# Four weight loads on one queue: moving a tap load and the projection load of a gated convolution to ScalarE's DMA queue

## The chip, the cores and the metric

The kernel runs on one core of a Trainium2 chip. A core has five engines with instruction streams of their own: TensorE (PE: matrix products into PSUM; its weight loads are shown apart, as PEld), VectorE (DVE), ScalarE (ACT), GpSimd (POOL) and SyncE (SP), which here only starts transfers. Transfers between HBM and the core's SBUF are done by 16 DMA engines. SyncE and ScalarE both start transfers in this kernel, each with an instruction in its own stream; the profile lists SyncE's transfers under the DMA queue q1 and ScalarE's under q10. The metric is the device time of one execution in microseconds (us), as the median of several runs.

## The reference

The inputs are `x` (2 x 16000 x 256, bf16), three taps `w` (3 x 256 x 512) and a projection `w_o` (256 x 256). It is a causal convolution over time with dilation 2, a gate and a projection:

```
h[t] = x[t] @ w[0] + x[t-2] @ w[1] + x[t-4] @ w[2]     (x before time 0 is zero)
f, g = the first and the last 256 columns of h
out  = (tanh(f) * sigmoid(g)) @ w_o
```

## The kernel before, in words

**Tiling.** Time is read in rows of four steps, t = 4r + j with j from 0 to 3, so that `x` of a batch has 4000 rows. A group is up to 256 such rows; there are 34 groups, and the first has 128 rows. Each group is made in four blocks of 128 output columns (two of f, two of g), 136 blocks in all. In SBUF `x` lies transposed (`xt`: input channels on the partitions, rows along the free dimension), because the products contract over channels. The steps j = 0, 1 of all rows of a block go to one PSUM bank (`a`), the steps j = 2, 3 to another (`b`).

**Two ways to a block.** The first group (blocks 0 to 3) is made directly: each bank adds the products of all three taps, tap 2 first, then tap 0, then tap 1 (`TAPS = (2, 0, 1)`, function `direct`, line 216). All later blocks use fewer products (function `products`, line 197): VectorE forms a difference `mm` (line 155) and a sum `pp` (line 161) of shifted rows, VectorE or GpSimd differences `dd` (line 172), and TensorE multiplies them by combined weights: `wm_sb` = w[0] + w[2] - w[1], `wp_sb` = w[0] + w[2] + w[1], and `wd0_sb`, `wd2_sb` = twice w[0] and w[2]. VectorE puts the results together (lines 234 and 235) after ScalarE has copied one bank (line 227). ScalarE applies tanh and sigmoid (line 248), VectorE multiplies them (line 266), TensorE projects with `wo_sb` (line 287), ScalarE evicts (line 306), and SyncE stores (line 308).

**How the combined weights come about.** ScalarE makes `wd0_sb` (line 363, needs w[0]) and `wd2_sb` (line 364, needs w[2]). VectorE makes `wt_sb` = w[0] + w[2] (line 365, needs those two), then `wm_sb` (line 366) and `wp_sb` (line 367), which need w[1] as well. Behind these three, in VectorE's stream, stand `mm` and `pp` of group 1 (lines 155, 161), which need the first transposed chunk.

**Loading.** `x` is loaded in chunks. The rows of chunk 0 (the first group) come as a plain copy (`xn`, line 117) and are transposed by TensorE with an identity (line 141); ScalarE and VectorE copy the result to `xt` (line 143, j even and j odd). All other chunks are loaded by a transposing DMA that SyncE starts (line 105). Chunk 1 has 256 rows and 16 rows of history (0.56 MB), chunk 2 and most others 512 and 16 (1.08 MB). Chunks 1 and 2 are started at once, since three buffers of `xt` are there; later ones wait for a buffer to come free. Each tap is 256 KB and `w_o` 128 KB, plain copies.

**The order at the start.** The kernel is in manual order: each engine runs its instructions as the text has them. At the start TensorE runs 28 small products on a zeroed tile (`warm_up`, line 92), then the transposes, one more small product, and the first group's products: 12 with tap 2, 12 with tap 0, 12 with tap 1 for blocks 0 to 2, then block 3's taps 2 and 0, the `wm` and `wp` products of block 4, and block 3's tap 1. ScalarE starts two tap loads (line 119), loads its activation table (line 120), and comes to its copies of line 143. SyncE starts `xn` (line 117), tap 0 (line 121) and then the transposing loads. The load of `w_o` is in ScalarE's stream behind its first activations of block 0 (line 375).

Of the kernel before, what the change touches and what calls it, by code (L numbers as in the profile page):

```python
# [13 lines left out]
def kernel(  # L14
# [19 lines left out]
    nc = tc.nc  # L34
# [4 lines left out]
    P = 128  # L39
# [7 lines left out]
    TAPS = (2, 0, 1)  # L47
# [41 lines left out]
    def warm_up(n):  # L89
        wps = ps_a.tile([P, 2 * RG], f32, name="a")  # L90
        for _ in range(n):
            nc.tensor.matmul(wps[:, :P], lhsT=warm[:], rhs=warm[:], start=True, stop=True)  # L92
# [20 lines left out]
    w_taps = [consts.tile([P, CT, D2], bf16, name=f"w{k}_sb") for k in range(K)]  # L113
    wo_sb = consts.tile([P, NT, D], bf16)
    xn = consts.tile([P, 4, D], bf16, name="xn")
    w_in = [w[k].rearrange("(ct c) d -> c ct d", c=P) for k in range(K)]
    nc.sync.dma_start(out=xn[:], in_=x[0, 0:4 * P, :].rearrange("(r j) c -> r j c", j=4))
    for k in (TAPS[0], TAPS[2]):
        nc.scalar.dma_start(out=w_taps[k][:], in_=w_in[k])
    nc.scalar.preload_act_table(ACT.Sigmoid)  # L120
    nc.sync.dma_start(out=w_taps[TAPS[1]][:], in_=w_in[TAPS[1]])
    warm_up(N_WARM[0])
    ident = consts.tile([P, P], bf16)
    make_identity(nc, ident[:])
# [56 lines left out]
    def products(k, which):  # L181
        g, oi = divmod(k, 4)
        G = groups[g]
        o = O_ORDER[oi]
        osl = slice(o * P, (o + 1) * P)
        R = G["R"]
        N = 2 * R
        if which in (1, 2):
            G["ab"[which - 1], oi] = (ps_a, ps_b)[which - 1].tile([P, 2 * RG], f32, name="ab"[which - 1])
        wmat, mv, bank, first = {  # L190
            2: (wm_sb, lambda ct: G["m"][:, :, ct, :R], "b", True),
            1: (wp_sb, lambda ct: G["p"][:, :, ct, :R], "a", True),
            3: (wd0_sb, lambda ct: G["d"][:, 2:4, ct, :R], "b", False),
            0: (wd2_sb, lambda ct: G["d"][:, 0:2, ct, :R], "a", False),
        }[which]
        for ct in range(CT):
            nc.tensor.matmul(  # L197
                G[bank, oi][:, :N], lhsT=wmat[:, ct, osl], rhs=mv(ct),
                start=first and ct == 0, stop=ct == CT - 1, skip_group_check=True,
            )  # L200
# [21 lines left out]
    def copy_m2(k):  # L222
        g, oi = divmod(k, 4)
        G = groups[g]
        N = 2 * G["R"]
        G["ss", oi] = ss_pool.tile([P, 2 * RG], f32, name="ss")
        nc.scalar.copy(out=G["ss", oi][:, :N], in_=G["b", oi][:, :N])  # L227
# [9 lines left out]
    def activate(k):  # L237
        g, oi = divmod(k, 4)
        G = groups[g]
        R = G["R"]  # L240
        o = O_ORDER[oi]
        if oi == 0:
            G["th"] = act_pool.tile([P, NT, 4, RG], bf16, name="th")
            G["sg"] = act_pool.tile([P, NT, 4, RG], bf16, name="sg")
            G["z"] = z_pool.tile([P, NT, 4, RG], bf16, name="zz")
        dst = G["th"][:, o] if o < NT else G["sg"][:, o - NT]
        for h, bank in ((1, "b"), (0, "a")):
            nc.scalar.activation(  # L248
                out=dst[:, 2 * h:2 * h + 2, :R],
                in_=G[bank, oi][:, :2 * R].rearrange("p (q r) -> p q r", q=2),  # L250
                func=ACT.Tanh if o < NT else ACT.Sigmoid, scale=1.0 if g == 0 else 0.5,
            )
# [118 lines left out]
    direct(3, TAPS[:-1])  # L371
    products(N_DIRECT, 2)
    products(N_DIRECT, 1)
    activate(0)
    nc.scalar.dma_start(out=wo_sb[:], in_=w_o.rearrange("(ct c) d -> c ct d", c=P))
    activate(1)
    activate(2)
    copy_m2(N_DIRECT)
    for part in range(3):
        last = pre_d(1, part, nc.vector)  # L380
# [8 lines left out]
    k = N_DIRECT + 1  # L389
# [76 lines left out]
```

## Time and profile before

| what | value |
|---|---|
| median of 3 runs (all) | 284.21 us (284.19, 284.21, 284.81) |
| the profiled execution | 284.75 us; its span 283.0 us |
| TensorE busy | 278.2 us, 98% of the span |
| ScalarE, VectorE, GpSimd busy | 261.2, 243.2, 126.2 us |
| bytes on SyncE's queue q1 and ScalarE's q10 | 33.59 MB and 0.66 MB |
| plain loads, from issue to landing (median) | taps on ScalarE 4.3 us, tap on SyncE 4.5 us, `xn` 2.9 us, `w_o` 4.1 us |
| transposing loads, from issue to landing (median) | 6.8 us |

The span is the time from the first to the last instruction in the profile; the profiled execution's own time is 1.75 us longer, for what lies around it. In a line of the timeline the first number is the start in us from the span's start and the second is how long it took; ACTq and SPq are the instructions by which ScalarE and SyncE start a transfer, which end when the transfer is handed over and not when the data has landed. In a line of a DMA queue the three numbers are packets, MB, and the packets' time as a share of 16 engines' time in the stretch; the share goes over 100% where packets overlap. A transposing load moves packets of 256 bytes, a tap load packets of 1 KB, `xn` of 2 KB, `w_o` of 512 bytes, and at the end of each transfer 4-byte packets set its semaphore.

### The profile page before, as it was taken

The page shows a single profiled execution, that of the slowest core. Times are in us where ns is not written, and L with a number is a line of the kernel's source. Part 1 is how long each engine was busy: PE and PEld are TensorE (multiplying, and loading weights), DVE is VectorE, ACT ScalarE, POOL GpSimd, SP SyncE. Part 2 cuts the span into 40 slices and gives each one's busy share as a digit, 9 for nine tenths or more (in the row PEclk, how much of TensorE's full clock was granted, in tenths as well). Part 3 has the DMA queues.
Part 4 walks back from the last instruction along what each step waited for, and adds up shares of the span by engine and source line. Part 5 has one row for each costly group of instructions (what it writes and reads, how often), then busy time and mean ns, then how long its engine had stood idle before and what let it go on. Part 6 is the DMA issues. An engine that isn't in the chain of part 4 may idle for free.

```text
span 283.0 us, 4903 instructions
## 1 busy us (share of the span) xinstructions
PE 278.2 (98%) x1641; PEld 160.5 (57%) x1641; DVE 243.2 (86%) x417; ACT 261.2 (92%) x533; POOL 126.2 (45%) x136
## 2 busy tenths in 40 slices
PE   8999999999999999999999999999999999999994
PEld 7645555555555555556854555555555555555782
DVE  2999888888888888888999988888888888888884
ACT  4699999999999999999999999999999999999994
POOL 1145455445444544543465544454445445443430
PEclk9999999999999999999999999999999999999999
DMA  8877191632828252182793714709355152321223
GB/s 206 195 174 168 58 210 74 153 113 82 182 76 151 88 115 75 41 222 76 177 257 96 166 41 122 179 37 171 127 124 149 45 156 76 79 75 74 76 87 110
DMA packets 76440, 34.55 MB, mean 122 GB/s; under 512 B 66944, under 2 KB 68480, under 8 KB 76416
## 3 DMA queue, kind: packets, MB, share of 16 engines
q1 hardware_dynamic: 75600, 33.59, 47.5%
q10 hardware_dynamic: 816, 0.66, 0.7%
q8 instruction: 13, 0.21, 0.3%
q14 instruction: 11, 0.09, 0.1%
HBM read 1.18 MB, written 16.38 MB: 62 GB/s over the span
## 4 chain that ended last, share of the span: by engine, by line
PE 98%; DVE 0%; DVEq 0%; issue 0%
PE a L197 38%; PE b L197 38%; PE o_ps L287 19%; PE a L216 1%; PE a L92 1%; PE b L216 1%; PE tp L141 0%; PE a L332 0%; DVE osb_end L339 0%; PE b L332 0%; DVEq L461 0%; DVE warm L112 0%
## 5 line engine op out<-in xcount | busy, mean ns | idle before, releaser
L172 POOL TENSOR_TENSOR dd<-xt 128x512 bf16<-128x512 bf16 (+2 forms) x128 | 125.4, 980 | 146.7 <-DVE zz L266 65.4
L234 DVE TENSOR_TENSOR b<-a,ss 128x512 f32<-128x512 f32 (+2 forms) x132 | 87.4, 662 | 30.9 <-ACT ss L227 27.8
L235 DVE TENSOR_TENSOR a<-a,ss 128x512 f32<-128x512 f32 (+2 forms) x132 | 86.2, 653 | 0.0
L227 ACT COPY ss<-b 128x512 f32<-128x512 f32 (+2 forms) x132 | 73.8, 559 | 11.9 <-PE b L197 1.1
L197 PEld LDWEIGHTS <-wd_sb 128*128 128x128 bf16 x528 | 51.4, 98 | 55.1 <-issue 0.6
L197 PE MATMUL a<-dd,wd_sb 128*128 128x512 bf16 (+2 forms) x264 | 74.7, 364 | 0.0
L197 PE MATMUL b<-mm,wm_sb 128*128 128x512 bf16 (+2 forms) x264 | 74.7, 364 | 0.0
L197 PE MATMUL a<-pp,wp_sb 128*128 128x512 bf16 (+2 forms) x264 | 74.7, 364 | 0.0
L197 PE MATMUL b<-dd,wd_sb 128*128 128x512 bf16 (+2 forms) x264 | 74.7, 364 | 0.0
L287 PE MATMUL o_ps<-wo_sb,zz 128*128 128x256 bf16 x488 | 73.2, 273 | 0.0
L306 ACT CAST osb<-o_ps 128x512 bf16<-128x512 f32 x121 | 71.9, 594 | 0.0
L287 PEld LDWEIGHTS <-zz 128*128 128x128 bf16 x488 | 47.7, 98 | 28.2
L266 DVE TENSOR_TENSOR zz<-th,sg 128x1024 bf16<-128x1024 bf16 (+1 forms) x67 | 43.1, 644 | 0.0
L248 ACT ACTIVATE th<-b 128x512 bf16<-128x512 f32 (+2 forms) x68 | 39.7, 584 | 2.0 <-PE b L216 1.4
L197 PEld LDWEIGHTS <-wp_sb 128*128 128x128 bf16 x264 | 25.8, 98 | 27.3
L248 ACT ACTIVATE sg<-b 128x512 bf16<-128x512 f32 (+2 forms) x68 | 39.6, 582 | 0.6 <-PE b L197 0.3
L248 ACT ACTIVATE th<-a 128x512 bf16<-128x512 f32 (+2 forms) x68 | 39.7, 584 | 0.0
L248 ACT ACTIVATE sg<-a 128x512 bf16<-128x512 f32 (+2 forms) x68 | 39.7, 583 | 0.0
L197 PEld LDWEIGHTS <-wm_sb 128*128 128x128 bf16 x264 | 25.8, 98 | 4.5
L161 DVE TENSOR_TENSOR pp<-xt 128x1024 bf16<-128x1024 bf16 (+2 forms) x33 | 21.9, 662 | 0.0
L155 DVE TENSOR_TENSOR mm<-xt 128x1024 bf16<-128x1024 bf16 (+2 forms) x33 | 21.5, 650 | 0.0
L216 PEld LDWEIGHTS <-w_sb 128*128 128x128 bf16 x48 | 4.9, 105 | 1.4 <-issue 0.2
(35 smaller groups left out, 37.5 us busy)
## 6 DMA issues: line engine op xcount, KB each, us to landing
out_dram<-osb SPq DMA_DIRECT2D x61, 256.0 KB, 2.1
w_sb<-in_w_dram ACTq DMA_DIRECT2D x2, 256.0 KB, 4.3
xt<-in_x_dram SPq DMA_TRANSPOSE x18, 6.8
xn<-in_x_dram SPq DMA_DIRECT2D x1, 256.0 KB, 2.9
w_sb<-in_w_dram SPq DMA_DIRECT2D x1, 256.0 KB, 4.5
out_dram<-osb_end SPq DMA_DIRECT2D x2, 128.0 KB, 1.9
wo_sb<-in_w_o_dram ACTq DMA_DIRECT2D x1, 128.0 KB, 4.1
out_dram<-osb_odd SPq DMA_DIRECT2D x8, 16.0 KB, 3.0
```

The costliest lines, as they stand in the source:

```text
L155: return nc.vector.tensor_tensor(out=G["m"][:, :, :, :G["R"]], in0=xc, in1=yp, op=ALU.subtract)
L161: return nc.vector.tensor_tensor(out=G["p"][:, :, :, :G["R"]], in0=xc, in1=yp, op=ALU.add)
L172: ins = eng.tensor_tensor(out=G["d"][:, j, :, :R], in0=a[:, q], in1=s[:, q], op=ALU.subtract)
L197: nc.tensor.matmul(G[bank, oi][:, :N], lhsT=wmat[:, ct, osl], rhs=mv(ct), start=first and ct == 0, stop=ct == CT - 1, skip_group_check=True,)
L216: nc.tensor.matmul(G[bank, oi][:, :2 * R], lhsT=w_taps[tap][:, ct, osl], rhs=mv[:, :, ct, :], start=tap == TAPS[0] and ct == 0, stop=tap = ...
L227: nc.scalar.copy(out=G["ss", oi][:, :N], in_=G["b", oi][:, :N])
L234: nc.vector.tensor_tensor(out=pb[:, :N], in0=pa[:, :N], in1=ss[:, :N], op=ALU.subtract)
L235: nc.vector.tensor_tensor(out=pa[:, :N], in0=pa[:, :N], in1=ss[:, :N], op=ALU.add)
L248: nc.scalar.activation(out=dst[:, 2 * h:2 * h + 2, :R], in_=G[bank, oi][:, :2 * R].rearrange("p (q r) -> p q r", q=2), func=ACT.Tanh if o ...
L266: return nc.vector.tensor_tensor(out=G["z"][:, dt, :, :full], in0=G["th"][:, dt, :, :full], in1=G["sg"][:, dt, :, :full], op=ALU.mult)
L287: nc.tensor.matmul(o_ps[:, q, :], lhsT=lhsT, rhs=wo_sb[:, dt, :], start=(dt == 0), stop=(dt == NT - 1),)
L306: copy(out=osb[:, 2 * jp:2 * jp + 2, :], in_=o_ps[:])
```

## The change

All three taps and `w_o` are loaded by ScalarE, in the order in which the taps are used (2, 0, 1, then `w_o`), ahead of the load of its activation table. SyncE starts `xn` and, as its next instruction, the first transposing load. The load of `w_o` is no longer between ScalarE's activations; these keep their order. The streams of TensorE, VectorE and GpSimd are unchanged.

```
@@ -115,10 +115,10 @@
     xn = consts.tile([P, 4, D], bf16, name="xn")
     w_in = [w[k].rearrange("(ct c) d -> c ct d", c=P) for k in range(K)]
     nc.sync.dma_start(out=xn[:], in_=x[0, 0:4 * P, :].rearrange("(r j) c -> r j c", j=4))
-    for k in (TAPS[0], TAPS[2]):
+    for k in TAPS:
         nc.scalar.dma_start(out=w_taps[k][:], in_=w_in[k])
+    nc.scalar.dma_start(out=wo_sb[:], in_=w_o.rearrange("(ct c) d -> c ct d", c=P))
     nc.scalar.preload_act_table(ACT.Sigmoid)
-    nc.sync.dma_start(out=w_taps[TAPS[1]][:], in_=w_in[TAPS[1]])
     warm_up(N_WARM[0])
     ident = consts.tile([P, P], bf16)
     make_identity(nc, ident[:])
@@ -371,10 +371,8 @@
     direct(3, TAPS[:-1])
     products(N_DIRECT, 2)
     products(N_DIRECT, 1)
-    activate(0)
-    nc.scalar.dma_start(out=wo_sb[:], in_=w_o.rearrange("(ct c) d -> c ct d", c=P))
-    activate(1)
-    activate(2)
+    for k in range(3):
+        activate(k)
     copy_m2(N_DIRECT)
     for part in range(3):
         last = pre_d(1, part, nc.vector)
```

More of the change, by code (lines that the diff above doesn't have):

```diff
@@ L117 @@
     nc.sync.dma_start(out=xn[:], in_=x[0, 0:4 * P, :].rearrange("(r j) c -> r j c", j=4))
-    for k in (TAPS[0], TAPS[2]):
+    for k in TAPS:
         nc.scalar.dma_start(out=w_taps[k][:], in_=w_in[k])
+    nc.scalar.dma_start(out=wo_sb[:], in_=w_o.rearrange("(ct c) d -> c ct d", c=P))
     nc.scalar.preload_act_table(ACT.Sigmoid)
-    nc.sync.dma_start(out=w_taps[TAPS[1]][:], in_=w_in[TAPS[1]])
     warm_up(N_WARM[0])
@@ L373 @@
     products(N_DIRECT, 1)
[L374 to L377, printed above, removed]
+    for k in range(3):
+        activate(k)
     copy_m2(N_DIRECT)
```

## The prediction, made before the result was known

> **What bounds the kernel.** I read the page's busy times and its chain first.
>
> ```profile
> PE 278.2 (98%) x1641; PEld 160.5 (57%) x1641; DVE 243.2 (86%) x417; ACT 261.2 (92%) x533; POOL 126.2 (45%) x136
> ...
> PE 98%; DVE 0%; DVEq 0%; issue 0%
> ```
>
> TensorE is busy from 0.99 us to the end, and the chain that ends last is TensorE and nothing else. In the list of waits TensorE waits once, 1.0 us at the start for the zeroed tile. So the change can win next to nothing: the chain in order of time has, in the first 16 us, two pieces longer than their kind (0.45 and 0.55 us where 0.43 is usual), 0.14 us together. What it can do is make TensorE wait. A wait at the start is not recovered, since TensorE has no later slack.
>
> Next, the transfers at the start: the timeline of the issues, then the DMA queues in short windows.
>
> ```profile
> 1.23 0.49 ACTq L119 DMA_DIRECT2D w_sb<-in_w_dram  x1
> ...
> 1.19 0.42 SPq L121 DMA_DIRECT2D w_sb<-in_w_dram  x1
> ...
> 1.66 4.63 SPq L105 DMA_TRANSPOSE xt<-in_x_dram  x1
> ...
> 6.34 4.30 SPq L105 DMA_TRANSPOSE xt<-in_x_dram  x1
> ...
> 9.07 0.37 ACTq L375 DMA_DIRECT2D wo_sb<-in_w_o_dram  x1
> ```
>
> The windows below are 3.1 to 3.5, 3.8 to 4.1, 4.6 to 4.9, 9.5 to 11.8 and 11.9 to 12.6 us; each line is the queue that moved nearly all of that window.
>
> ```profile
> q10 hardware_dynamic: 137, 0.14, 99.1%
> ...
> q1 hardware_dynamic: 104, 0.11, 102.1%
> ...
> q10 hardware_dynamic: 98, 0.10, 97.4%
> ...
> q1 hardware_dynamic: 2606, 0.67, 127.5%
> ...
> q10 hardware_dynamic: 272, 0.13, 67.6%
> ```
>
> The reader is to see two things. First, the queues do not share the DMA engines; transfers go one behind the other in the order of their issue: `xn` (packets 1.7 to 3.0), tap 2 (2.7 to 3.8), tap 0 (3.5 to 4.7), tap 1 (4.1 to 5.3, stragglers to 5.8), first transposing load T1 (4.9 to 7.6, thus 2.7 us), second one T2 (7.7 to 12.2, thus 4.5 us). Secondly, `w_o` was issued by ScalarE at 9.07, in the middle of T2, and in 2.3 us after 9.5 only q1 moved anything; the first packets of `w_o` start at 11.9, when T2 runs out. A plain copy issued by ScalarE behind the start of a transposing load waited here until that load was through. This is the one place of the trace where that can be seen, and the changed kernel makes it the rule at the start.
>
> Last, the engines' timeline for who needs the taps.
>
> ```profile
> 1.75 1.28 ACT L120 ACT_TABLE_LOAD   x1 [1.75 <-issue]
> ...
> 5.77 1.22 DVE L365 TENSOR_TENSOR wt_sb<-w_sb 128x1024 f32<-128x1024 bf16 x1 [0.43 <-DMA w_sb<-in_w_dram]
> ...
> 7.03 1.23 DVE L366 TENSOR_TENSOR wm_sb<-wt_sb,w_sb 128x1024 bf16<-128x1024 f32 x1
> ...
> 9.91 0.69 DVE L161 TENSOR_TENSOR pp<-xt 128x1024 bf16<-128x1024 bf16 x1
> ...
> 11.08 0.59 PE L197 MATMUL a<-pp,wp_sb 128*128 128x512 bf16 x2
> ```
>
> VectorE runs without a gap from 5.77 (tap 0 landed at 1.19 + 4.5 = 5.69) to the end of `pp` at 10.60, and TensorE takes `pp` at 11.08. So this string of five instructions has less than half a microsecond of slack against TensorE, and it hangs on tap 0 and, from `wm_sb` on, on tap 1 (landed at 1.23 + 5.1 = 6.33, needed at 7.03).
>
> **The change, part by part.**
>
> *ScalarE's issues.* Two more ahead of the table load: one of 0.49 us (row of line 119) and one of 0.37 (line 375), with 0.03 between. The table load moves from 1.75 to about 2.67 and ends at 3.95. Behind it stands ScalarE's copy of line 143, which starts at 4.41 because of TensorE. Cost nothing, with 0.46 us of cover; if ScalarE is held at an issue, all above that 0.46 falls on TensorE's first product (5.06), which needs these copies. The issue taken out at 9.07 frees 0.37 us of ScalarE, which runs beside TensorE there: nothing.
>
> *SyncE's issues.* Tap 0's 0.42 us goes; T1 moves up from 1.66 to 1.19, and T2 follows as soon as T1's issue is done. `xn` is issued as before and lands at 3.64 as before; TensorE's warm-up ends at 4.16 and hides it.
>
> *Tap 2* is issued at 0.74 as before, lands at 4.34, is needed at 5.06: nothing.
>
> *Tap 0* moves from SyncE (1.19) to ScalarE (1.23), 0.04 us behind T1's issue instead of 0.47 us ahead of it. Which goes first? `xn` shows 0.96 us from the start of a copy's issue to its first packet (0.74 to 1.7); the third transposing load, started alone at 12.77, has its first packets at 14.0, 1.2 us. So tap 0 would be ready at 2.2 and T1 at 2.4, both behind tap 2. I take tap 0 first, by 0.2 us: cost nothing. The other end, T1 first, is the second case below.
>
> *Tap 1* moves from 1.23 to about 1.75, ready at 2.7, behind T1 by 0.3 us. By the row of `w_o` it then waits for all of T1. T1 starts when tap 0 ends, about 4.5, and takes 2.7 us: 7.2, less 0.1 for the overlap between transfers: 7.1. From first packet to landing tap 2 took 1.6 us (2.75 to 4.34), tap 1 2.2. Tap 1 now lands at 8.7 with the shorter, since nothing else is in flight beside it at first; 9.3 with the longer. `wm_sb` moves from 7.03 to 8.7, 1.67 later, and the string behind it as much: `mm` ends at 11.67, `pp` at 12.27. TensorE needs tap 1 itself at 8.42: it waits 0.3, and is ready for `wm_sb`'s product at 10.98 instead of 10.65; it then waits for `mm` to 11.7, and for `pp` to about 12.3 where it started at 11.08. Path: +1.2 us. With landing at 9.3 it is +1.8; with T1 in 2.2 us (the unhindered issue of the 304-row chunk took 2.55, which makes 2.3 for T1's 272 rows) +0.6. A gain is excluded as an end here, since tap 1 cannot land ahead of a queue it joins later.
>
> *`w_o`* goes behind tap 1, 0.7 us of transfer (11.9 to 12.6), landing near 10 if T2 is behind it and near 14 if not; its first use is 15.55: nothing.
>
> *T1 and T2.* T1's last packets were at 7.6, it landed at 1.66 + 7.1 = 8.77, and `mm` read it at 9.31; ending at 7.2 it lands by 8.4, ahead of the later `mm`: nothing. T2 landed at 6.34 + 7.2 = 13.5 for group 2's `mm` at 14.97. Behind tap 1 (7.1 to 8.0) and `w_o` (to 8.6) its 4.5 us end at 13.1, and it lands at 14.4; that `mm` has itself moved by 1.2: nothing, but this is the next to be late, from another 1.8 us on.
>
> Sum: the profiled execution's 284.75 plus 1.2 is 285.95. That execution lies 0.54 above the median of the runs shown; the median plus 1.2 is 285.4. I say 285.7, between the two.
>
> The Trainium skill bears on the row of `w_o` from two sides; nothing above hangs on it. "Perfetto Trace Analysis", section on the HWDGE DMA instruction, says that the generator of descriptors is shared and is locked by one instruction until all its descriptors are made, and that the profiled time of an issue holds the wait for this lock. The wait of `w_o`'s data agrees; its issue of 0.37 us inside T2's 4.30 shows no such wait. "DMA: Bandwidth & Descriptors", section on queues, rings and completion order, says the opposite for the data: that each DMA engine takes turns between queues, 9 to 17 descriptors typically and at most 64 a turn. The row differs: 2606 packets of q1 are 163 per engine without one turn for q10.
>
> **The rivals.**
>
> *T1 goes before tap 0.* For it: 0.04 us between the issues, T1 the earlier. Against: the transposing load's longer way to its first packet. T1 then runs from 3.7 to 6.4, tap 0 from 6.3, landing at 7.9, tap 1 0.65 later. `wt_sb` moves from 5.77 to 7.95, and the string by 2.2: `pp` ends at 12.8, TensorE's `pp` product moves by 1.8, with the longer landing by 2.4: 286.0 to 287.1.
>
> *T2 too goes before tap 1.* In the start of the kernel before, the queues alternate (q1, q10, q1, q10). If they take turns by whole transfers, tap 1 or tap 0 gets one turn after T1 and the rest waits for T2: 4.5 + 2.6 + 4.5 puts tap 1's packets at 11.6 and its landing at 13.3. `wm_sb` moves by 6.3, TensorE's `pp` product from 11.08 to about 17.0: +5.9 to 6.5, 290.1 to 291.3. For it: `w_o` found no turn inside T2, and T2's issue follows T1's by 0.05 us. Against: `w_o` does not show what happens between two transposing loads. TensorE would idle for 4 us and might start again at its first pace (six products took 1.38 us at 5.1, later 0.65): up to 2.7 us more.
>
> *ScalarE is held at an issue*, since four transfers stand in its queue. The tail on SyncE has one issue of 1.7 us behind four others. Held until T1's issue is done, near 4.5, TensorE's first product moves by 2: 286.2 to 286.9.
>
> *Not slower: the copies pass T1.* `w_o` waited because a transposing load was already streaming; at 1.2 to 2.6 us none is, all transfers wait behind `xn` and tap 2, and the three copies may all be queued before T1's first packet. It decides if T1 is ready later than tap 1, that is 0.3 us later than I take it. Then the order is that of before with `w_o` put in, T1 lands within 0.3 us of before, and VectorE starts up to 0.6 us earlier, worth at most the 0.14 us: 284.1 to 284.8. The turn-taking rule of "DMA: Bandwidth & Descriptors" in the Trainium skill would lead to this case as well.
>
> **How the numbers follow.** One chunk late with tap 0 ahead: 0.33. T1 before tap 0: 0.17. T2 before tap 1: 0.22. ScalarE held: 0.05. Copies pass: 0.20. Something that wins over 0.3%, against the chain: 0.03. The likeliest is the first, 285.7, its own range 284.8 to 286.6 (0.6 to 1.8 on either base). The range from 284.1 to 290.8 holds all but half of the T2 case and most of the last: some 0.85. Within 0.3% (0.85 us, about what a measurement of this kernel can tell from no change): the passing case and the first one's lower end, 0.20. Faster 0.04, slower 0.76.
>
> **What would show it.** Right: in the changed profile tap 1's packets on q10 start only after T1's last, near 7; `wm_sb` waits for a DMA until 8.7; TensorE has waits of about 1 us for VectorE between 10 and 12.5, and nothing else moves. Wrong: q10 packets for all taps before T1's (no loss), `wt_sb` waiting as well (T1 first), tap 1 landing past 12 (T2 first), or the table load ending after 4.4 (ScalarE held).

## The result, and the profile after

The changed kernel takes 286.54 us as the median of 22 executions, the kernel before 284.58 us in 22 executions beside it. The ratio is 1.0065 with a 95% interval of 1.0045 to 1.0085 (a ratio taken by batches of runs; the two medians alone make 1.0069): slower by 0.45 to 0.85%. More telling than the median is the spread. The kernel before stays between 284.05 and 285.02 us; the changed one goes from 284.51 to 288.34, so some executions lose nothing and some lose almost 4 us.

The first profile of the changed kernel is of an execution that lost nothing (284.72 us, span 282.9). These are its page's busy times and chain:

```profile
PE 278.2 (98%) x1641; PEld 160.6 (57%) x1641; DVE 243.1 (86%) x417; ACT 261.4 (92%) x533; POOL 126.2 (45%) x136
...
PE 98%; DVE 0%; DVEq 0%; issue 0%
```

Its timeline (start, duration, engine, line, what) shows the string that hangs on the taps:

```profile
2.79 1.28 ACT L121 ACT_TABLE_LOAD   x1 [2.79 <-issue]
...
5.38 1.23 DVE L365 TENSOR_TENSOR wt_sb<-w_sb 128x1024 f32<-128x1024 bf16 x1
...
7.12 1.23 DVE L366 TENSOR_TENSOR wm_sb<-wt_sb,w_sb 128x1024 bf16<-128x1024 f32 x1 [0.51 <-DMA w_sb<-in_w_dram]
...
11.08 0.59 PE L197 MATMUL a<-pp,wp_sb 128*128 128x512 bf16 x2
```

The table load ends at 4.07, ahead of ScalarE's copies at 4.41, as before. Tap 0 is there earlier (`wt_sb` at 5.38 instead of 5.77), but `wm_sb` now waits 0.51 us for tap 1 and starts at 7.12, a tenth later than before. VectorE's slack takes that up: TensorE's `pp` product is at 11.08 in both. The DMA queues of the same execution, from 4.3 to 5.9, 5.4 to 6.5 and 7.1 to 7.9 us (packets, MB, share of 16 engines):

```profile
q1 hardware_dynamic: 1085, 0.28, 79.8%
q10 hardware_dynamic: 227, 0.22, 40.4%
...
q10 hardware_dynamic: 269, 0.26, 69.8%
q1 hardware_dynamic: 438, 0.11, 45.6%
...
q10 hardware_dynamic: 262, 0.13, 85.3%
q1 hardware_dynamic: 246, 0.05, 35.7%
```

The first transposing load T1 starts at 4.3 behind taps 2 and 0. At 5.9, when half of tap 1's packets have started, 1085 of T1's 2176 packets have gone, 68 for each of the 16 DMA engines. So tap 1 is moved between 5.4 and 6.5, in the middle of T1, and most of `w_o` from 7.1 on, at T1's end. (The trace does not say which DMA engine moved a packet, so a number of packets per engine is a mean over all 16.)

### The profile page after: what moved, and what is told of

It is laid out like the page before. It is cut to its first block, busy times and chain, and to the rows that moved or that the text cites. A ratio compares the mean times of both kernels' runs of the same rounds, so it can differ in the third digit from the quotient of the medians.

```text
span 282.9 us, 4902 instructions
## 1 busy us (share of the span) xinstructions
PE 278.2 (98%) x1641; PEld 160.6 (57%) x1641; DVE 243.1 (86%) x417; ACT 261.4 (92%) x533; POOL 126.2 (45%) x136
## 3 DMA queue, kind: packets, MB, share of 16 engines
HBM read 1.18 MB, written 16.38 MB: 62 GB/s over the span
## 4 chain that ended last, share of the span: by engine, by line
PE 98%; DVE 0%; DVEq 0%; issue 0%
PE a L197 38%; PE b L197 38%; PE o_ps L287 19%; PE a L216 1%; PE a L92 1%; PE b L216 1%; PE tp L141 0%; PE a L332 0%; DVE osb_end L339 0%; PE b L332 0%; DVEq L459 0%; DVE warm L112 0%
```

## The experiments

T1 and T2 are the first and the second transposing load. In all experiments the question is when a copy that ScalarE issues gets its place among T1's packets, and what that costs TensorE.

**1. The changed kernel once more, for a longer execution.** No edit.

> The changed kernel once more, unaltered, to see its spread and, with luck, a profile of a slower execution. In the profile seen so far TensorE waits for nothing and tap 1's data go in among the packets of the first transposing load T1. Theory (the copies that ScalarE issues behind the start of T1 race with its stream for the DMA engines, and how late tap 1 lands differs from execution to execution): times scattered over 284.5 to 288.3 us; a profile over 286 us shows wm_sb waiting for tap 1's transfer by 1 us or more beyond 7.1 us, and TensorE waiting for VectorE by the amount that the execution is longer. Rival (ScalarE held at an issue): in such a profile the table load ends after 4.4 us and the first product starts late. Rival (second transposing load late): the mm at 15 us waits for a transfer.

Measured: median 286.56 us of 6 executions (285.61 to 288.23), ratio 1.0077 (1.0053 to 1.0101). The profiled execution took 286.82 us (span 285.0). First the chain of this execution in order of time (start, duration, what), then its waits (us in total, times, longest):

```profile
1.75 7.65 DMA w_sb<-in_w_dram
...
9.49 1.23 DVE wm_sb L366
10.72 1.14 DVE wp_sb L367
11.85 0.62 DVE mm L155
...
12.52 0.60 PE b L197 x2
```

```profile
DVE wm_sb L366 <- DMA w_sb<-in_w_dram: 2.9, 1, 2.9
...
PE a L216 <- DMA w_sb<-in_w_dram: 0.9, 1, 0.9
...
PE b L197 <- DVE mm L155: 0.7, 1, 0.7
PEld L197 <- DVE pp L161: 0.5, 1, 0.5
```

Tap 1 is issued at 1.75 and lands 7.65 us later, at 9.40. `wm_sb` starts at 9.49, TensorE waits 0.9 us for the tap itself, 0.7 for `mm` and 0.5 for `pp`, and its `pp` product is at 13.12 instead of 11.08: 2.04 us, and the span is 2.0 us longer than that of before. ScalarE's table load is at 2.79 again and its copies at 4.41, so it was not held; the `mm` of T2's chunk had no wait for a transfer. Both of these rivals fall.

**2. Only tap 0 moved.** The kernel before with tap 0 on ScalarE's queue; the load of `w_o` stays in its old place.

```
-    for k in (TAPS[0], TAPS[2]):
+    for k in TAPS:
         nc.scalar.dma_start(out=w_taps[k][:], in_=w_in[k])
     nc.scalar.preload_act_table(ACT.Sigmoid)
-    nc.sync.dma_start(out=w_taps[TAPS[1]][:], in_=w_in[TAPS[1]])
```

> The changed kernel with the load of w_o back between ScalarE's activations; only tap 0 has moved to ScalarE. Theory (tap 1 is late behind T1): as slow as the changed kernel, mean near 286 us with the same scatter. Rival (w_o ahead of the table load is what costs): back to 284.6 us with the scatter of the kernel before.

Measured: median 286.11 us (284.46 to 288.23, 12 executions), ratio 1.0058 (1.0033 to 1.0083): the whole loss and the whole spread without `w_o`'s move. Its profiled execution (286.95 us) is another long one, `wm_sb` at 9.53. Since `w_o` is not in the way here, q10 shows where tap 1 is late; this is the window from 7.0 to 8.9 us:

```profile
q1 hardware_dynamic: 1373, 0.34, 141.4%
q10 hardware_dynamic: 48, 0.03, 7.0%
```

A tap is 0.26 MB, 16 KB on each DMA engine. The 0.03 MB of q10 in this window are as much as the shares of two engines out of 16; nearly all the rest of tap 1 had gone by 7.0. Its last packet starts at 8.77. The 4-byte packets at its end, 16 as there are DMA engines, agree: 14 have started by 7.31, the last two start at 8.47 and 8.82. T1's own last 4-byte packets start at the same times (28 of 32 by 7.89, the others at 8.47 and 8.82), so both loads seem to be late on the same two engines. The tap lands with its slowest engine.

**3. Only `w_o` moved.** The kernel before with `w_o` as ScalarE's third load.

```
     for k in (TAPS[0], TAPS[2]):
         nc.scalar.dma_start(out=w_taps[k][:], in_=w_in[k])
+    nc.scalar.dma_start(out=wo_sb[:], in_=w_o.rearrange(...))
     nc.scalar.preload_act_table(ACT.Sigmoid)
...
     activate(0)
-    nc.scalar.dma_start(out=wo_sb[:], in_=w_o.rearrange(...))
```

> The kernel before with nothing but the load of w_o moved: third on ScalarE, ahead of the table load; tap 0 stays on SyncE ahead of T1. Theory: 284.6 us, within 0.3 us of the kernel before, since taps 0 and 1 are both issued ahead of T1, and w_o, even if it waits for T1, is not needed before 15.5 us. Rival (w_o's move costs): 286 us.

Measured: median 284.65 us (284.26 to 284.94, 12 executions), ratio 1.0004 (0.9996 to 1.0013). No difference: the move of `w_o` and the later table load cost nothing, as forecast. The trace shows one thing more. `w_o` is ScalarE's third load here and its issue begins 0.08 us after T1's (1.74 against 1.66), yet its packets start at 4.92, ahead of T1's at 5.30. It did not wait for T1 at all.

**4. T1 held back until ScalarE has handed over its copies.** All loads as in the changed kernel.

```
         if c == 0:
             return
+        if c == 1:
+            nc.gpsimd.memset(xt[:, 0:2, :, RH:RH + XW - RH], 0.0)
```

> The changed kernel, with a fill of chunk 1's buffer by GpSimd, some 1.3 us from 1.4 us on, that T1 has to wait for, so that it is issued near 2.7 us, when ScalarE has handed over its last copy. Theory: all copies go ahead of T1, no wait of wm_sb, 284.6 us and the narrow scatter of the kernel before. Rival (ScalarE's queue with four copies, or its later table load): as slow as the changed kernel, near 286 us, since ScalarE's issues are the same.

Measured: median 284.88 us (284.34 to 285.34, 11 executions), ratio 1.0013 (1.0004 to 1.0022). T1 is issued at 3.06 us instead of 1.20, and nearly all of the loss and of the spread is gone. The timeline of VectorE:

```profile
5.26 1.22 DVE L367 TENSOR_TENSOR wt_sb<-w_sb 128x1024 f32<-128x1024 bf16 x1
6.50 1.23 DVE L368 TENSOR_TENSOR wm_sb<-wt_sb,w_sb 128x1024 bf16<-128x1024 f32 x1
...
9.05 0.70 DVE L157 TENSOR_TENSOR mm<-xt 128x1024 bf16<-128x1024 bf16 x1 [0.18 <-DMA xt<-in_x_dram]
```

`wm_sb` follows `wt_sb` without a wait. ScalarE's four issues are where they were in the changed kernel, so it is the order of T1 and the copies that decides, not ScalarE's queue. What T1 loses shows as well: `mm` waits 0.18 us for it.

**5. Tap 1 behind `w_o`.** ScalarE's third and fourth load exchanged.

```
-    for k in TAPS:
+    for k in TAPS[:2]:
         nc.scalar.dma_start(out=w_taps[k][:], in_=w_in[k])
     nc.scalar.dma_start(out=wo_sb[:], in_=w_o.rearrange(...))
+    nc.scalar.dma_start(out=w_taps[TAPS[2]][:], in_=w_in[TAPS[2]])
```

> The changed kernel with ScalarE's third and fourth load exchanged: taps 2 and 0, w_o, tap 1. Theory now (ScalarE's queue gets turns inside the transposing load, one transfer a turn, after every 64 descriptors per DMA engine, so that its third transfer comes after the first 64 of T1's 136 and its fourth after 128): w_o takes the turn near 5.3 us that tap 1 had, tap 1's packets come at 7.2 us and after in every execution, wm_sb starts between 8.7 and 10.5 us and the time is 286.0 to 288, without the fast executions of the changed kernel. Rival (a copy waits until the whole transposing load is through, as the prediction had it): w_o and tap 1 both after T1's last packets, none of them inside T1. Rival (tap 1 gets in at any place by chance): scatter as in the changed kernel, from 284.5.

Measured: median 286.50 us (285.86 to 287.48, 4 executions), ratio 1.0090 (1.0067 to 1.0114); no short execution among them, which four executions hardly prove: of the 28 of the changed kernel (22 and the 6 of experiment 1), 7 lie under 285.5. The profile says more. The DMA queues from 4.3 to 5.7 and from 6.7 to 7.5 us:

```profile
q1 hardware_dynamic: 1114, 0.29, 90.1%
q10 hardware_dynamic: 225, 0.15, 32.5%
...
q10 hardware_dynamic: 250, 0.25, 90.4%
q1 hardware_dynamic: 165, 0.04, 22.4%
```

Now `w_o` goes in the middle of T1 (half of its packets have started at 5.69, with T1 at 69 packets per engine), and tap 1 takes the place at T1's end. `wm_sb` is at 8.37, a little before the range that I gave. So the place in the queue counts: with this T1, third means its middle and fourth its end. It does not count alone, since the third load of experiment 3 went ahead of a T1 that was issued later. The expectation's 128 packets per engine was wrong; all 2176 packets of T1, 136 per engine, had started when half of tap 1's had.

**6. Tap 1 issued late.** Behind ScalarE's copies of line 143, at 4.73 us.

```
-    for k in TAPS:
+    for k in TAPS[:2]:
         nc.scalar.dma_start(out=w_taps[k][:], in_=w_in[k])
...
     for j in range(4):
         turn(j)
+    nc.scalar.dma_start(out=w_taps[TAPS[2]][:], in_=w_in[TAPS[2]])
```

> The changed kernel with tap 1 issued by ScalarE behind its copies of line 143, near 5.2 us, when T1's issue is done or nearly done and T2's begins. Theory of turns: tap 1 gets a turn after at most 64 descriptors per engine that are already set in order, about 1.5 us of data, plus 64 more: packets between 7.5 and 9.5 us, wm_sb at 9 to 11, 286 to 288.5 us. Rival (a copy waits for the whole transposing load, here T2, to near 12 us): wm_sb near 13 us and 290 us or more.

Measured: median 286.73 us (286.46 to 287.98, 4 executions), ratio 1.0096 (1.0071 to 1.0120). In the profile tap 1's packets start at 7.56, at the end of T1, and `wm_sb` at 10.07; T2 follows. A wait for the whole of T2 (290 us) did not come. Tap 1 was issued when T1 had just begun to stream (T1's first packet is at 4.32), and waited for T1's end.

**7. Tap 1 in two halves.**

```
+    for ct in range(CT):
+        nc.scalar.dma_start(out=w_taps[TAPS[2]][:, ct], in_=w_in[TAPS[2]][:, ct])
```

(in place of its one load, behind taps 2 and 0)

> The changed kernel with tap 1 loaded in two halves of 128 KB, one behind the other on ScalarE. Theory of turns: the first half takes the turn after T1's first 64 descriptors per engine, the second the one after 128, near 7.2 us: every execution is late, 285.5 to 288, median above that of the changed kernel or equal to it with no execution under 285. Rival (it is bandwidth shared with T1, or chance in one slow engine): the same bytes, the same 284.5 to 288.3 and the same median.

Measured: median 285.68 us (285.27 to 286.58, 4 executions), ratio 1.0054 (1.0035 to 1.0074). No execution is under 285 us, as forecast by turns, but four executions cannot show that (24 of the 28 of the changed kernel are over 285 as well). The second half's packets do come at T1's end (`wm_sb` at 8.39 in the profile). The median is below that of the changed kernel, which neither side had forecast; with 4 executions I make nothing of that.

**8. Taps 0 and 1 exchanged.**

```
-    for k in TAPS:
+    for k in (TAPS[0], TAPS[2], TAPS[1]):
```

> The changed kernel with taps 0 and 1 exchanged on ScalarE's queue: 2, 1, 0, w_o. Theory (the third place on the queue is what is late, whatever stands in it): tap 0's packets start inside T1 at 5.3 us, wt_sb starts between 7.1 and 9.5 us instead of 5.4; with the string of five VectorE instructions behind it TensorE loses the start minus 6.2 us: 0.9 to 3.3, 285.4 to 288, every execution slower than the kernel before. Rival (tap 1's own load is slow): tap 1 late again, time as in the changed kernel.

Measured: median 288.38 us (287.11 to 289.01, 4 executions), ratio 1.0140 (1.0112 to 1.0167). `wt_sb` waits 4.07 us for tap 0 and starts at 9.40. Every execution is slow: whatever stands third here is late, and tap 0 there costs more, since `wt_sb` stands ahead of `wm_sb` in the string. The loss is above the forecast; the last section comes back to it.

**9. T1 in two transposing loads of half the columns each.**

```
-        nc.sync.dma_start_transpose(out=xt[:, :, :, ...], in_=x[...])
+        halves = ((0, 2), (2, 4)) if c == 1 else ((0, 4),)
+        for j0, j1 in halves:
+            nc.sync.dma_start_transpose(out=xt[:, j0:j1, :, ...], in_=x[...][:, j0 * D:j1 * D])
```

> The changed kernel with T1 cut into two transposing loads of half the columns each (68 tiles of 4 KB, 68 packets of 256 bytes per DMA engine, instead of 136). Theory A (queue q10 gets a turn at the middle and at the end of each transposing load): tap 1 after 34 packets per engine, that is near 4.9 us instead of 5.3, w_o near 5.6; median nearer the kernel before, 284.6 to 285.6. Theory B (a turn after 64 packets, however long the load): tap 1 near 5.3 us as in the changed kernel, w_o before 7 us instead of 7.2; times as in the changed kernel, 284.5 to 288. Theory C (the place is set by when ScalarE's issue falls in T1's issue): tap 1 near 5.3 us, too.

Measured: median 285.19 us (284.54 to 285.57, 7 executions), ratio 1.0023 (1.0011 to 1.0036). The DMA queues from 4.2 to 6.5 us:

```profile
q10 hardware_dynamic: 252, 0.24, 61.3%
q1 hardware_dynamic: 1090, 0.28, 60.4%
```

At 6.5 half of tap 1's packets have started, with T1 at 68 packets per engine, not 34, so the middle of a load has no part in it (theory A falls). But 68 is also the whole first half of T1, and its second half was issued at 2.57, after tap 1 (1.74) and `w_o` (2.26): in this run the transfers go in the order of their issue, and it cannot tell a turn after 64 packets from that order. The time, though, came out where A had it: here tap 1's last packet starts at 7.00, and it has no stragglers at 8.8. That short loads bound the stragglers is a reading of one profile and of the narrower spread, not more.

**10. T1 twice as long.**

```
-        cuts = [1, 1] if b == 0 else []
+        cuts = [1, 2] if b == 0 else []
```

> The changed kernel with 512 rows instead of 256 in chunk 1 (264 packets per engine in T1 instead of 136; later chunks are cut elsewhere). T1 itself then lands late, near 11.5 us for the mm that stood at 9.4, so the time is 2 us longer or more for that reason; what is asked is the place of tap 1. Theory A (turn at the middle): tap 1's packets start after 132 per engine, 6.4 to 6.6 us. Theories B and C (after 64, or set by the time of issue): they start near 5.3 us as in the changed kernel.

Measured: 287.65 us in 2 executions, with `mm` at 12.01 waiting for T1, as forecast. The DMA queues from 4.4 to 6.3 us:

```profile
q1 hardware_dynamic: 1238, 0.32, 86.7%
q10 hardware_dynamic: 213, 0.20, 32.3%
```

At 6.3 half of tap 1's packets have started, and T1 is at 77 of its 264 packets per engine. The middle would be 132. So the third transfer's place, near 70 packets per engine, hardly grows with T1. T1's queue from 4.4 to 8.85, when half of the packets of `w_o`, the fourth transfer, have started:

```profile
q1 hardware_dynamic: 2387, 0.61, 91.5%
```

That is 149 of T1's 264 packets per engine (the packets of `w_o` are spread from 6.6 to 10.6), so the fourth transfer's place is not tied to T1's end either.

**What the profiles give together.** In experiment 1 TensorE's `pp` product comes 3.63 us after the start of `wm_sb` (13.12 less 9.49). Before, it stood at 11.08, so TensorE should lose the start of `wm_sb` less 7.45 us. Each row is one profiled execution; the last column is its span less the 283.0 of before.

| kernel | `wm_sb` starts, us | start less 7.45 | span's difference |
|---|---|---|---|
| changed, first profile | 7.12 | none | -0.1 |
| 9, T1 in two | 7.89 | 0.44 | 0.4 |
| 5, tap 1 behind `w_o` | 8.37 | 0.92 | 0.9 |
| 7, tap 1 in halves | 8.39 | 0.94 | 0.9 |
| 1, changed again | 9.49 | 2.04 | 2.0 |
| 2, only tap 0 moved | 9.53 | 2.08 | 2.1 |
| 6, tap 1 late | 10.07 | 2.62 | 3.2 |

The spans of this list follow tap 1's landing to 0.1 us, but for the last, which the last section takes up.

## Why the prediction was right or wrong

*Slower, by a late tap 1: right.* The place, the string behind it and TensorE's three waits (tap, `mm`, `pp`) are as the prediction's first case had them, with tap 0 ahead of T1. Experiments 2, 3 and 4 show it from three sides: tap 0's move alone brings the loss, `w_o`'s move alone nothing, and holding T1 back takes it away.

*The size: forecast +1.2, measured +1.96 between the medians.* The term that was off is tap 1's landing: 8.7 in the sum, with 9.3 as the later end; 9.40 in the long execution of experiment 1, where the loss was 2.04 and the prediction's later end gave 1.8. The price of lateness after that was right. Two numbers of the working were off without consequence: T1 in 2.3 us gives about +0.8 (a landing at 8.3), where the lower end has +0.6, and the first packet of `xn` starts at 1.77 and not at 1.7.

*The step that failed: "by the row of `w_o` it then waits for all of T1".* It does not. Most of tap 1 goes in the middle of T1, after about 68 packets per engine, and in the first profile all of it; then nothing is lost. Late are the shares of one or two engines that come at T1's end. I had made one forecast for all executions; in truth the executions differ, 7 of the 22 below 285.7 and 15 above. So it is in part luck that the median lies within the first case's range: a tap that waits for all of T1 on every engine was reckoned to land at 8.7 to 9.3, and a tap that is late on one or two engines landed at 9.4 in experiment 1. What had misled me is the one row of `w_o`, handed over 2.7 us after T2's issue began and 1.3 us after T2's first packet: such a copy came at T2's end (its first packet at 11.94, when 4126 of T2's 4224 packets had started; in experiment 2 again, at 12.47), and so did tap 1 of experiment 6 at T1's. Copies handed over ahead of T1's first packet can get places inside. The Trainium skill's rule that each DMA engine takes turns between queues, at most 64 descriptors at a time ("DMA: Bandwidth & Descriptors", on queues, rings and completion order), which I had set against that row, is near to the 68 to 77 packets per engine measured here for tap 1, with T1 of 136 and of 264. It does not explain the row of `w_o`, nor why the fourth transfer comes at 136 packets, or near 149, and not at 128.

*The rivals.* T1 ahead of tap 0: no; tap 0's packets start at 3.83, T1's at 4.33. T2 ahead of tap 1: no; even tap 1 issued at 4.73 came ahead of T2. ScalarE held at an issue: no; its issues take 0.46 to 0.49 us each and the table load ends at 4.07 (forecast 3.95). The copies pass T1: not as described, since T1 starts ahead of tap 1; but its time, 284.1 to 284.8, is that of the shortest executions.

*The parts costed at nothing* stayed so: `w_o` (experiment 3), the table load, tap 2, T2 (its chunk's `mm` at 14.97 as before).

*Open:* why in some executions one or two DMA engines bring tap 1 last, and what fixes the 68 packets. Experiments 9 and 10 rule out the middle of the load; a fixed turn and the time at which ScalarE's issue falls in T1's issue were not told apart. Experiment 3 speaks for the time (its third load, issued 0.08 us after T1, went ahead of T1), experiments 5 and 6 against it (their fourth loads, issued at 2.26 and 4.73, both came at T1's end). Whether the late engines had tap 1 further back in their order or were slow in all they did is open too: in experiment 2 T1 is late on them as well.

## What to carry to other kernels

A small load that something waits for should be handed over ahead of a long transposing load, also of one on another queue; here ScalarE's queue did not shield a tap from a load on SyncE's, and being issued 0.5 us behind that load instead of 0.4 us ahead of it cost 2 us at the median. A transfer lands with the last of its DMA engines, so look for its last packet and not for its mean rate, and take the spread of executions before a single profile: this kernel's first profile showed no loss at all. If the order of issues cannot be kept, holding the long load back until the small ones are handed over gave nearly all of the loss back.

## What the runs showed of the hardware that was not expected

A short wait of TensorE can cost twice. In experiment 8 it waited from 6.7 to 9.3 us for tap 0. These are stretches of that profile (stretch; length; busy time and instructions of PE, PEld, DVE, ACT, POOL; granted clock; DMA share; GB/s):

```profile
5.40:8.70 3.30, 1.26 (x12) 0.86 (x9) 0.00 (x0) 0.00 (x0) 0.00 (x0) 1.00 1.23 167
8.80:12.10 3.30, 2.75 (x13) 1.96 (x14) 2.66 (x3) 2.00 (x2) 0.00 (x0) 0.50 1.26 227
12.20:15.50 3.30, 3.30 (x28) 2.51 (x27) 3.05 (x7) 2.35 (x7) 0.17 (x1) 1.00 0.65 145
```

In experiment 6 it waited for 2.2 us, to 10.0, resumed at full clock, and fell to half 1.3 us later, while it was working:

```profile
7.90:11.20 3.30, 1.18 (x11) 1.05 (x12) 1.13 (x1) 0.53 (x2) 0.00 (x0) 1.00 1.22 236
11.30:14.60 3.30, 3.30 (x14) 1.65 (x13) 3.30 (x6) 1.52 (x6) 0.00 (x0) 0.50 0.69 155
14.70:18.00 3.30, 3.30 (x18) 1.66 (x17) 2.97 (x6) 2.54 (x7) 1.04 (x1) 1.00 0.20 43
```

The trace has the clock at half from 8.73 to 12.15 and from 11.27 to 14.68, 3.41 us each time, and in the 3.3 us ahead of that TensorE was busy for 1.26 and 1.18 us. Experiment 8 lost 3.5 us by its span, where the late start of `wt_sb` alone gives 3.2 by the rule of its expectation (9.40 less 6.2), and experiment 6 has 0.6 us more than the late `wm_sb` explains; the half clock is the likely reason, but no run takes it away. In experiments 1 and 2 TensorE waited for about 2 us in several pieces and was busy for 2.4 to 2.7 us in the stretches of 3.3 to 3.4 us with these waits; the clock stayed at 1.00. The Trainium skill ("TensorE: Matmul & The Clock Gate", on the clock gate) has a window of 3.4 us that runs on its own and halves the clock after an idle one. The length of the slow stretches agrees, but here a stretch that was idle for some 2.1 us of 3.3 was enough.
